# Retention, Fourier mixing and feed-forward on one core: half-height score pairs, and all queues behind the first batch ordered by due times computed in the program text

## Chip, cores and metric

One Trainium2 chip, one core of it. The metric is device time in microseconds (us), fast runs only. Before: 247.51 us, median of 3 (247.45 to 247.79). Engine names as in the profile: PE = TensorE, PEld = its weight loads, DVE = VectorE, ACT = ScalarE, POOL = GpSimd, SP = SyncE, which here issues nearly all the DMAs. A line number such as L1114 is a line of the kernel whose profile is shown; the same statement has another number in each kernel.

## The reference

Four batches, eight heads, 768 rows, heads of 64. Retention with a decayed state, then a two-dimensional Fourier transform (real part), a normalisation, and a feed-forward part of width 2048.

```python
gamma = 1.0 - 2.0 ** (-5.0 - np.arange(H))
for t in range(S):
    state = gamma * state + einsum('bhd,bhe->bhde', k[:, :, t], v[:, :, t])
    y[:, :, t] = einsum('bhd,bhde->bhe', q[:, :, t], state) / np.sqrt(D)
# x: the heads side by side, (4, 768, 512)
u = x + np.real(np.fft.fft(np.fft.fft(x, axis=1), axis=2))
un = (u - mean(u)) / np.sqrt(var(u) + 1e-06)
out = u + np.maximum(un @ w_ch1, 0.0) @ w_ch2          # 512 -> 2048 -> 512
```

## The kernel before

The kernel works on heads in pairs and on rows in six chunks of 128, in fp16 with fp32 sums. While the feed-forward matmuls of one batch run, the retention of the next lies between them. The score unit, with cuts marked:

```python
def a_unit(b, i, part):                      # three parts for each pair of heads
    def run():
        ...                                  # cut: allocation of atm
        wk = ps_g.tile([P, 2, 2, P], f32, tag="g", name="wkA")
        for c2 in range(2):
            c = 2 * part + c2                # qT is zero-padded: both heads in one matmul of 256 columns
            mm = nc.tensor.matmul(wk[:, c2], st["kT"][:, c, :], st["qT"][:, :, c, :], start=True, stop=True)
        nc.vector.tensor_tensor(out=st["atm"][:, 2 * part:2 * part + 2], in0=wk, in1=maskp[...], op=ALU.mult)
```

The casts of batches three and four on GpSimd. `qzs` has two buffers, used in turn, so the cast of the third pair has to wait for the DMA transpose that reads the first pair's buffer, and the fourth for the second:

```python
q16 = qzs[i % 2]
for h2 in range(2):
    nc.gpsimd.tensor_scalar(out=q16[:, h2, :, D * h2:D * h2 + D], in0=q32[:, h2], scalar1=1.0, scalar2=1.0, ...)
...                                          # cut: two casts of k (kd), one of v; later SP transposes q16 to qT
```

The order of the queues comes from the framework's scheduler with hand-set pins:

```python
def pin(engines=None):                       # chain the new instructions of these engines in program order
    for n in range(mark[0], len(ins)):
        ...                                  # cut
        tc.add_manual_dep(x, tails[e], ..., reason="pinned order")
...                                          # cut
...                                          # cut: if e[0] < 1.0, that is, in the first part of the schedule alone
pin(None if e[0] < 0.05 else ["Pool", "GpSimd"])   # first units: all engines; then GpSimd alone
```

Of the kernel before, what the change touches and what calls it, by code (L numbers as in the profile page):

```python
# [31 lines left out]
FB = 1  # L32
NPE = 2
ACT_ROWS = ((2, 5, 6, 7, 8, 9, 10, 14), (0, 3, 6, 7, 9, 10, 11, 12, 14, 15), (2, 4, 5, 6, 7, 8, 10, 14))


@with_exitstack
def kernel(
# [56 lines left out]
    tails, base = {}, {}  # L95
    mark = [0]

    def pin(engines=None):
        ins = tc.nc.cur_bb.bb.instructions
        for n in range(mark[0], len(ins)):  # L100
            x = ins[n]
            e = str(x.engine)
            if engines is not None and not any(g in e for g in engines):
                continue
            if e in tails:
                tc.add_manual_dep(x, tails[e],
                                  mybir.DependencyInfo(mybir.DependencyClass.NoSync,
                                                       mybir.DependencyReason.DATA),
                                  reason="pinned order")
            tails[e] = x.name  # L110
        mark[0] = len(ins)

    def behind():
        for x in tc.nc.cur_bb.bb.instructions[mark[0]:]:
            if str(x.engine) in base:
                tc.add_manual_dep(x, base[str(x.engine)],
                                  mybir.DependencyInfo(mybir.DependencyClass.NoSync,
                                                       mybir.DependencyReason.DATA),
                                  reason="behind the first batch")

    def held(unit):
        def run():
            ins = tc.nc.cur_bb.bb.instructions
            n0 = len(ins)
            unit()
            for n in range(n0, len(ins)):
                m = n - 1
                while m >= 0 and ins[m].engine != ins[n].engine:
                    m -= 1
                if m >= 0:  # L130
                    tc.add_manual_dep(ins[n], ins[m].name,
                                      mybir.DependencyInfo(mybir.DependencyClass.NoSync,
                                                           mybir.DependencyReason.DATA),
                                      reason="casts in turn")
        return run

# [15 lines left out]
    def load_unit(b, i, after=None):  # L152
        def run():
            h0 = 2 * PAIR_ORDER[i]
            for name, src in srcs.items():
                t = inp.tile([P, 2, NCH, D], f32, tag="in32", name=f"{name}32")
                rows = "h (p c) d -> p h c d" if b < NPE and name == "q" else \
                    "h (c p) d -> p h c d"
                dma = nc.sync.dma_start(t, src[b, h0:h0 + 2].rearrange(rows, p=P))  # L159
                if after is not None:  # L160
                    for x in (w_dma[after].ins, lb[0]["mm"].ins):
                        tc.add_manual_dep(dma.ins, x.name,
                                          mybir.DependencyInfo(mybir.DependencyClass.Sync,
                                                               mybir.DependencyReason.DATA),
                                          reason="loads in turn")
                if b > 1:
                    tc.add_manual_dep(dma.ins, a_of[b - 1, 1].ins.name,
                                      mybir.DependencyInfo(mybir.DependencyClass.Sync,
                                                           mybir.DependencyReason.DATA),
                                      reason="loads behind the transposes")  # L170
                in_of[name, b, i] = t
        return run
# [56 lines left out]
    def late_consts():  # L229
        with tc.issue_after(lb[0]["una"].ins):  # L230
            for h in range(H):
                nc.scalar.activation(maskp[:, h // 2, h % 2], maskf, AF.Copy, bias=0.0,
                                     scale=float(gam[h] ** (-P)))
# [119 lines left out]
    at, q16_of, kd_of, v16_of, last_cast = {}, {}, {}, {}, {}  # L353

    def cast_unit(b, i):
        def run():
            h0 = 2 * PAIR_ORDER[i]
            q32, k32, v32 = (in_of.pop((n, b, i)) for n in "qkv")
            kd = kp.tile([P, NCH, 2, D], f16, tag="kd16", name="kd16")
            v16 = vp.tile([P, NCH, 2, D], f16, tag="v16", name="v16")  # L360
            with ExitStack() as es:
                if b < NPE:
                    if (b, i - 1) in last_cast:
                        es.enter_context(tc.issue_after(last_cast[b, i - 1].ins))
                    q16 = qzs[i % 2].rearrange("p h c d -> p (h c d)")[
                        :, 0:NCH * P].rearrange("p (c h d) -> p c h d", c=NCH, h=2)
                    es.enter_context(tc.issue_after(nc.gpsimd.tensor_scalar(
                        out=q16, in0=q32.rearrange("p h c d -> p c h d"), scalar1=1.0,
                        scalar2=1.0, op0=ALU.mult, op1=ALU.mult).ins))
                else:  # L370
                    q16 = qzs[i % 2]
                    for h2 in range(2):
                        dst = q16[:, h2, :, D * h2:D * h2 + D]
                        nc.gpsimd.tensor_scalar(out=dst, in0=q32[:, h2], scalar1=1.0,
                                                scalar2=1.0, op0=ALU.mult, op1=ALU.mult)
                for h2 in range(2):
                    kc = nc.gpsimd.tensor_scalar(out=kd[:, :, h2, :], in0=k32[:, h2],  # L377
                                                 scalar1=gkd[:, h0 + h2:h0 + h2 + 1],
                                                 scalar2=1.0, op0=ALU.mult, op1=ALU.mult)
                    if b < NPE:  # L380
                        es.enter_context(tc.issue_after(kc.ins))
                last_cast[b, i] = nc.gpsimd.tensor_scalar(  # L382
                    out=v16, in0=v32.rearrange("p h c d -> p c h d"), scalar1=1.0, scalar2=1.0,
                    op0=ALU.mult, op1=ALU.mult)
            q16_of[b, i], kd_of[b, i], v16_of[b, i] = q16, kd, v16
        return run
# [25 lines left out]
    def v0_unit(i):  # L412
        def run():
# [3 lines left out]
            last_cast[0, i] = nc.gpsimd.tensor_scalar(  # L417
# [168 lines left out]
    def a_unit(b, i, part):  # L586
        def run():
            st = at[b, i]
            if part == 0:
                st["atm"] = ap_.tile([P, NCH, 2, P], f16, tag="atm", name="atm")  # L590
            wk = ps_g.tile([P, 2, 2, P], f32, tag="g", name="wkA")
            for c2 in range(2):
                c = 2 * part + c2
                mm = nc.tensor.matmul(wk[:, c2], st["kT"][:, c, :], st["qT"][:, :, c, :],  # L594
                                      start=True, stop=True)
            a_of[b, i] = mm
            nc.vector.tensor_tensor(  # L597
                out=st["atm"][:, 2 * part:2 * part + 2], in0=wk,
                in1=maskp[:, PAIR_ORDER[i]].unsqueeze(1).to_broadcast([P, 2, 2, P]),
                op=ALU.mult)  # L600
# [399 lines left out]
    def attn_steps(b):  # L1000
        steps = []
        for step in range(6):
            un = []
            if step < 4:
                un.append(held(cast_unit(b, step)))
# [13 lines left out]
            if 0 <= i < 4:  # L1019
                if b == 0:  # L1020
                    un += [a0_unit(b, i, 0), a0_unit(b, i, 1)]
                else:
                    un += [a_unit(b, i, part) for part in range(3)]
# [62 lines left out]
    def emit(streams):  # L1086
# [5 lines left out]
        for e in ev:  # L1092
            e[3]()
            if e[0] < 1.0:
                behind()
                pin(None if e[0] < 0.05 else ["Pool", "GpSimd"])

    pin()
    for u in first_units():
        u()  # L1100
        pin()
    base.update(tails)
# [4 lines left out]
    for b in range(B):  # L1107
# [14 lines left out]
        dm = (0.12, 0.24, 0.3, 0.38) if b == 0 else (0.004, 0.140, 0.232, 0.341)  # L1122
        streams += [(majors, b, b + 1.0), (s2s, b + dm[0], b + dm[1]),
                    (unTs, b + dm[2], b + dm[3])]
        if b + 1 < B:
            steps = attn_steps(b + 1)
            if b == 0:
                streams.append(([load_unit(1, i, 6) for i in range(4)], 0.180, 0.220))
                streams.append(([qt_zeros], 0.1, 0.15))
                streams.append(([half_tables], 0.655, 0.655 + 0.02))  # L1130
                streams.append(([pad_unit], 0.673, 0.703))
                ts = (0.249, 0.368, 0.410, 0.415, 0.507, 0.615, 0.680, 0.685)
            else:
                streams.append(([load_unit(b + 1, i) for i in range(4)], b + -0.370, b + 0.075))
                n = [len(u) for u in steps[1:]]
                ts = [-0.040, -0.020] + [0.050 + 0.585 * sum(n[:j]) / sum(n)
                                         for j in range(6)]
# [3 lines left out]
            da = (0.062, 0.080, 0.173, 0.203, 0.271, 0.321) if b == 0 else \  # L1141
                (0.063, 0.067, 0.048, 0.158, 0.168, 0.189)
# [4 lines left out]
    emit(streams)  # L1147

# [29 lines left out]
```

## Time and profile before

| | before |
|---|---|
| time, median of fast runs | 247.65 us (4 runs of the same rounds as after) |
| span of the profiled run, mean granted clock | 246.0 us, 1.000 |
| PE busy | 234.4 us, 95% |
| PE time lost against each matmul form's median interval | 14.8 us, of it 9.9 before 36 us and 5.0 behind |

The last row is read from the start times of single matmuls: interval from one start to the next, less the median interval of the same form, added up where it is above 40 ns. It counts waits, mode switches and half-speed stretches alike, and is the measure used below.

The prediction shows the page and the stages. One more stage matters for what followed, the change from batch three to batch four, here on the timelines of POOL and SP (columns: start, length, engine, line, operation, tiles, shapes, count, and in brackets the idle time before and what ended it):

```profile
140.03 0.64 POOL L866 TENSOR_TENSOR u<-u,x 128x256 f32<-128x256 f32 x1
140.64 0.98 POOL L374 TENSOR_SCALAR q16z<-q 128x384 f16<-128x384 f32 x2
```

```profile
137.86 3.61 SPq L910 DMA_TRANSPOSE unT<-un  x2
141.65 1.44 SPq L542 DMA_TRANSPOSE qTz<-q16z  x1
```

The reader is to see two orders. POOL does the additions that end batch three's transform (u) first and batch four's next q cast afterwards. SP transposes batch three's normalised rows (unT), which the feed-forward part waits for, ahead of batch four's heads (qTz).

### The profile page before, as it was taken

The numbers are of one execution on the slowest core, as the hardware profiler recorded it, in microseconds if no ns is written. First come the engines' busy times: TensorE is split into PE (matmuls) and PEld (weight loads), VectorE is DVE, ScalarE is ACT, GpSimd is POOL, SyncE is SP. The second block draws the span as 40 slices with busy tenths as digits, with TensorE's granted clock in tenths as the row PEclk, the third lists the DMA queues.
The fourth block names the chain that finished last, engine by engine and source line by source line (L and its number), as shares of the span: only waits on it lengthen the run. The fifth ranks groups of instructions, "written<-read, shape, count | busy, mean of one in ns | idle before, by whom it ended". The sixth has DMA issues, their size and how long they took to land.

```text
span 246.0 us, 5309 instructions
## 1 busy us (share of the span) xinstructions
PE 234.4 (95%) x2024; PEld 144.4 (59%) x2024; DVE 177.5 (72%) x430; ACT 124.3 (51%) x276; POOL 81.3 (33%) x146
## 2 busy tenths in 40 slices
PE   6897899999999999999999999999999998999994
PEld 2454668956676655665567446665666455445543
DVE  8998957898788788995987648887895657424122
ACT  8798669477785445742247415732257217202500
POOL 6667600376500068690001637660003214000000
PEclk9999999999999999999999999999999999999999
DMA  8998999699999287988999589596100331121012
GB/s 174 257 260 138 200 204 206 152 250 261 275 233 214 56 171 176 190 174 149 242 266 210 119 183 181 108 138 150 58 0 3 60 133 30 38 85 43 0 45 85
DMA packets 99209, 36.39 MB, mean 148 GB/s; under 512 B 89840, under 2 KB 96240, under 8 KB 99184
## 3 DMA queue, kind: packets, MB, share of 16 engines
q1 hardware_dynamic: 94960, 31.86, 62.5%
q0 software_dynamic: 4224, 4.19, 10.5%
q8 instruction: 16, 0.26, 0.5%
q14 instruction: 9, 0.07, 0.1%
HBM read 27.26 MB, written 6.29 MB: 136 GB/s over the span
## 4 chain that ended last, share of the span: by engine, by line
PE 72%; DVE 8%; POOL 7%; ACT 4%; SPq 3%; DMA 2%; issue 2%; POOLq 0%; DVEq 0%
PE psc L973 30%; PE psh L930 23%; SPq L159 3%; PE ps L730 3%; PE psh L947 3%; PE wkA L594 3%; DMA k<-in_k_dram 2%; PE wkY L648 2%; POOL u L864 2%; POOL u L866 2%; PE wkY L644 1%; DVE bst L883 1%; PE wkK L613 1%; DVE u L834 1%; PE pq L827 1%
## 5 line engine op out<-in xcount | busy, mean ns | idle before, releaser
L973 PE MATMUL psc<-w,ht 128*128 128x512 f16 (+1 forms) x400 | 89.6, 370 | 0.1
L930 PE MATMUL psh<-unT,w 128*128 128x384 f16 x448 | 81.3, 326 | 0.6 <-ACT ht L934 0.6
L973 PEld LDWEIGHTS <-ht 128*128 128x128 f16 x400 | 38.1, 98 | 35.5 <-issue 0.3
L930 PEld LDWEIGHTS <-w 128*128 128x128 f16 x448 | 42.3, 98 | 24.9 <-issue 1.3
L934 ACT ACTIVATE ht<-psh 128x384 f16<-128x384 f32 x64 | 30.6, 488 | 39.4 <-PE psh L930 38.3
L864 POOL TENSOR_TENSOR u<-u,x 128x256 f32<-128x256 f32 x21 | 13.3, 634 | 102.3 <-DVE u L834 90.7
L977 DVE SCALAR_TENSOR_TENSOR ob<-psc,stats,u 128x512 f32<-128x512 f32 (+1 forms) x25 | 18.1, 722 | 27.4 <-PE psc L973 27.3
L936 DVE TENSOR_SCALAR ht<-psh 128x384 f16<-128x384 f32 x48 | 26.3, 551 | 8.6 <-PE psh L930 8.3
L597 DVE TENSOR_TENSOR atm<-wkA,maskp 128x512 f16<-128x512 f32 x36 | 23.9, 685 | 1.0 <-PE wkA L594 1.0
L885 ACT ACTIVATE un<-u,stats 128x512 f16<-128x512 f32 x21 | 15.1, 721 | 16.9 <-DVE stats L884 8.7
L883 DVE BATCH_NORM_STATS2 bst<-u 128x6 f32<-128x512 f32 x21 | 14.6, 694 | 9.7 <-POOL u L866 9.5
L623 DVE SCALAR_TENSOR_TENSOR s<-s,gk,wkK 128x128 f16<-128x128 f16 x48 | 16.4, 343 | 2.3 <-ACT s L619 1.4
L656 ACT ACTIVATE x<-wkY,gexp 128x384 f16<-128x384 f32 x24 | 12.8, 580 | 9.3 <-PE wkY L648 9.3
L145 PE MATMUL wps<-ht 128*128 128x512 f16 x40 | 13.3, 439 | 2.2 <-POOL ht L196 2.2
L377 POOL TENSOR_SCALAR kd<-k,gexp 128x384 f16<-128x384 f32 x24 | 13.8, 584 | 2.4 <-DMA k<-in_k_dram 2.4
L866 POOL TENSOR_TENSOR u<-u,x 128x256 f32<-128x256 f32 x21 | 13.3, 634 | 2.8 <-DVE u L837 1.5
L594 PE MATMUL wkA<-qTz,kT 128*128 128x256 f16 x72 | 13.6, 273 | 0.0
L829 ACT COPY qn<-pq 128x128 f32<-128x128 f32 x18 | 4.9, 274 | 14.1 <-PE pq L827 13.9
L947 PE MATMUL psh<-unT,w 128*128 128x128 f16 x192 | 11.5, 219 | 0.1
L947 PEld LDWEIGHTS <-w 128*128 128x128 f16 x192 | 11.0, 98 | 0.7 <-issue 0.5
L382 POOL TENSOR_SCALAR v<-v 128x768 f16<-128x768 f32 x12 | 10.0, 830 | 2.0 <-DMA v<-in_v_dram 1.9
L594 PEld LDWEIGHTS <-kT 128*128 128x128 f16 x72 | 6.9, 98 | 6.0 <-DVE s L623 0.4
(164 smaller groups left out, 318.2 us busy)
## 6 DMA issues: line engine op xcount, KB each, us to landing
q<-in_q_dram SPq DMA_DIRECT2D x16, 384.0 KB, 6.2
k<-in_k_dram SPq DMA_DIRECT2D x16, 384.0 KB, 5.6
v<-in_v_dram SPq DMA_DIRECT2D x16, 384.0 KB, 6.6
out_dram<-ob SPq DMA_DIRECT2D x23, 256.0 KB, 2.6
w<-in_moe_w_ch_dram POOLq DMA_DIRECT2D x8, 512.0 KB, 11.1
out_dram<-ob SPq DMA_DIRECT2D x2, 128.0 KB, 1.7
unT<-un SPq DMA_TRANSPOSE x15, 2.4
qTz<-q16z SPq DMA_TRANSPOSE x8, 3.8
```

The source lines that it names most:

```text
L594: mm = nc.tensor.matmul(wk[:, c2], st["kT"][:, c, :], st["qT"][:, :, c, :], start=True, stop=True)
L597: nc.vector.tensor_tensor(out=st["atm"][:, 2 * part:2 * part + 2], in0=wk, in1=maskp[:, PAIR_ORDER[i]].unsqueeze(1).to_broadcast([P, 2, 2, ...
L623: nc.vector.scalar_tensor_tensor(out=s16[:, c], in0=s16[:, c - 1], scalar=gk2[:, hp:hp + 1], in1=wk[:, c - c0], op0=ALU.mult, op1=ALU.add)
L864: nc.gpsimd.tensor_tensor(out=u[:, kb, 0:256], in0=u[:, kb, 0:256], in1=x[:, kb, 0, 1:257], op=ALU.add)
L866: nc.gpsimd.tensor_tensor(out=u[:, kb, 256:512], in0=u[:, kb, 256:512], in1=x[:, kb, 1, 257:1:-1], op=ALU.add)
L883: nc.vector.bn_stats(bst, u[:, kb, :])
L930: nc.tensor.matmul(psh, w116[:, cb, fb * P:(fb + 1) * P], unT[:, cb, rt * 384:(rt + 1) * 384], start=(cb == 0), stop=(cb == 3))
L934: nc.scalar.activation(ht16[:, fb, :], psh, AF.Relu, bias=0.0, scale=-1.0)
L936: nc.vector.tensor_scalar(out=ht16[:, fb, :], in0=psh, scalar1=-1.0, scalar2=0.0, op0=ALU.mult, op1=ALU.max)
L947: mm = nc.tensor.matmul(psh[:, f], w116[:, cb, fb * P:(fb + 1) * P], unT[:, cb, kb * P:(kb + 1) * P], start=(cb == 0), stop=(cb == 3))
L973: nc.tensor.matmul(psc[:, c0:c1], ht16[:, fb, rb3 * P:(rb3 + 1) * P], w216[:, fb, c0:c1], start=(fb == 0), stop=(fb == NFB - 1))
L977: nc.vector.scalar_tensor_tensor(out=ob[:, c0:c1], in0=psc[:, c0:c1], scalar=lb[b]["st"][:, rb, 3:4], in1=lb[b]["u"][:, rb, c0:c1], op0=AL ...
```

## The change

Two intents. First, the scores of two heads become two concurrent matmuls of 64 rows: a pair of them takes 52 to 56 ns from start to start in the traces, a zero-padded matmul of 256 columns 109 ns. Second, the hand-set pins go; the program text itself gives each instruction a cost and a due time, worked backwards from PE's program order, simulates the five queues and pins the order that comes out. With the second goes a set of new tables (LD1 and others) of where in the program each unit of work stands; no run tried these alone. The core of the diff, the rest cut:

```diff
+SLACK = 12000.0
+BY_DUE = ('PE', 'DVE', 'Activation', 'Pool', 'SP')
+def instr_cost(x, PSUM=PSUM):
+    ...                                     # cut
+    if eng == "PE":
+        ...                                 # cut: n columns written; half, if an operand has at most 64 rows
+        return max(n / 2.4 + 2.5, 27.0) * (0.5 if half else 1.0), n / 2.4 + 165.0
+    if kind == "InstDMACopy":
+        return (780.0 if eng == "Pool" else 400.0), None       # time the issuing engine is taken, ns
+    if kind == "InstDmaTransposeAnt":
+        return 1400.0, 3800.0 if el > 600 else 2450.0
+    ...                                     # cut
+def order_queues(tc, told, kept):
+    ...                                     # cut: who needs whom; due times backwards
+    rank = [(due[n] if eng[n] in BY_DUE else float(n), n) for n in range(len(ins))]
+    ...                                     # cut: simulated queues take the ready instruction of lowest rank
+            rate = 205.0 if e == "Pool" else 225.0 if runs[-1][1] <= 64 else 340.0
+            dma = max(dma, t + 1300.0) + 4.0 * size / rate
+            end = dma + 600.0
+    ...                                     # cut: every queue is pinned to that order
-    def pin(engines=None): ...              # and behind(), held(): removed
     def a_unit(b, i, part):                 # now two parts for each pair
-            wk = ps_g.tile([P, 2, 2, P], f32, tag="g", name="wkA")
-            for c2 in range(2):
-                c = 2 * part + c2
-                mm = nc.tensor.matmul(wk[:, c2], st["kT"][:, c, :], st["qT"][:, :, c, :], ...)
+            wk = [ps_g.tile([P, 3, P], f32, tag="g", name="wkA", padded_shape=[P, 4, P]) for _ in range(2)]
+            for c3 in range(3):
+                c = 3 * part + c3
+                for h2 in range(2):
+                    sl = slice(D * h2, D * h2 + D)
+                    mm = nc.tensor.matmul(wk[h2][:, c3, :], st["kT"][sl, c, :], st["qT"][sl, h2, c, :], ...)
```

## The prediction

> **What bounds the kernel now.** In the names, psh and psc are the two layers of the feed-forward part and fill most of PE's time; tq are transposes, wkA scores, wkK states, wkY the attention's output; ps, pq the Fourier part; pst turns the normalised un into unT. I read the page first, then the windows view cut at the stages, then groups by shape, the PE timeline, and the start times of single matmuls.
>
> ```profile
> PE 234.4 (95%) x2024; PEld 144.4 (59%) x2024; DVE 177.5 (72%) x430; ACT 124.3 (51%) x276; POOL 81.3 (33%) x146
> PE 72%; DVE 8%; POOL 7%; ACT 4%; SPq 3%; DMA 2%; issue 2%; POOLq 0%; DVEq 0%
> ```
>
> TensorE is busy 95% of the span and has 72% of the chain that ended last. The stages say it more sharply:
>
> ```profile
> 41.20:59.00 17.80, 17.80 (x211) 13.42 (x211) 14.92 (x43) 12.57 (x23) 9.92 (x15) 1.00 1.04 215
> 59.00:82.50 23.50, 23.28 (x246) 15.26 (x244) 20.21 (x46) 15.04 (x29) 4.89 (x8) 1.00 1.12 230
> 82.50:135.00 52.50, 51.98 (x442) 32.91 (x440) 43.42 (x109) 25.23 (x60) 19.31 (x33) 1.00 0.95 184
> 135.00:187.50 52.50, 52.10 (x415) 31.54 (x414) 40.07 (x96) 22.70 (x54) 18.82 (x33) 1.00 0.56 111
> 187.50:243.00 55.50, 54.62 (x312) 29.69 (x310) 23.56 (x49) 15.84 (x38) 7.02 (x12) 1.00 0.18 56
> ```
>
> The first two numbers are the length and PE's busy time: behind the first batch 199.8 of 201.8 us. Taking each matmul's start to the next one's start, and the median of its form as its cost, I find 4.2 us of lost time in that stretch. So order alone can win 4.2 us at the very most, plus about 1 us at 34 to 41 us. A win of 2% is 5 us. Two of the losses:
>
> ```profile
> 95.12 0.44 PE L613 MATMUL wkK<-v,kd 128*128 128x128 f16 x5 [0.47 <-POOL v L382]
> 208.03 3.41 PE L930 MATMUL psh<-unT,w 128*128 128x384 f16 x20 [0.44 <-ACT ht L934]
> ```
>
> **What the Trainium skill says.** "TensorEngine Tiling (Array Packing)", Key Properties: a change of tiling mode drains TensorE. The trace agrees. The first batch already forms its scores with 64-row matmuls, between full-height fillers:
>
> ```profile
> 17.87 0.60 PE L145 MATMUL wps<-ht 128*128 128x512 f16 x2
> 18.41 0.51 PE L458 MATMUL wkA<-qTz,kT 64*128 64x128 f16 x12
> 18.85 0.39 PE L145 MATMUL wps<-ht 128*128 128x512 f16 x1
> ```
>
> Fillers follow each other at 216 ns, so two take 0.43 us, but the 64-row burst starts 0.54 us after them: single starts show 312 ns in place of 216, so 96 ns on entry, in two bursts alike (others enter 96 to 97 ns late behind other forms). On leaving, the next matmul starts 149 ns after the last half matmul where 53 is its own time: 96 ns again. The first pair and the first filler lose 10 ns more each. "TensorE: Matmul & The Clock Gate", The mechanism (part 3): matmuls in different row groups start some 4 ns apart and all matmuls keep program order. The trace agrees: the partners start 3 to 4 ns apart, pairs 52 to 56 ns apart. The same page, Architectural detail, says that ScalarE and VectorE are strict FIFO; nothing in the trace contradicts it, and the stages below rest on it.
>
> **Part 1, half-height pairs.** Removed: 72 full-height matmuls.
>
> ```profile
> L594 PE MATMUL wkA<-qTz,kT 128*128 128x256 f16 x72 | 13.6, 273 | 0.0
> L597 DVE TENSOR_TENSOR atm<-wkA,maskp 128x512 f16<-128x512 f32 x36 | 23.9, 685 | 1.0 <-PE wkA L594 1.0
> ```
>
> The 13.6 us include overlap; from start to start one takes 109 ns, together 7.9 us. Added: 144 of half height, 72 pairs. At 53 ns a pair and nothing else, 3.8 us: 4 us saved, which the new cost function in the program assumes (half the time, no switch). But the built order shows where they stand: in batch two three bursts of 12, one of 6 and two of 3 matmuls; in batches three and four sixteen bursts of 6, each between full-height matmuls. A burst costs 56 ns a pair plus 0.21 us for the switches: 0.55 us (12), 0.38 (6), 0.32 (3, two pair slots). Sum: 3 x 0.55 + 17 x 0.38 + 2 x 0.32 = 8.75 us. **Part 1 costs about 0.9 us** on the path. The evictions become 48 of 384 columns in place of 36 of 512; 685 less 128 columns at about 1 ns makes 0.55 us each, 26 us in place of 24: DVE is beside the path, no charge.
>
> **Part 2, the order at 48 to 66 us.** In the new program all 48 psc matmuls of the first half of batch one stand before the first transposes (tq) of batch two; before, 20 stood ahead and the rest lay between them. They go in fours by the w2 load that they need, and the reason is in the program text: its cost function charges each weight load 4 bytes x 262144 / 205 = 5.1 us. The trace has the packets of those eight loads at 2.6 to 3.7 us each, done at 44.8 us, and the batch-two loads start right behind:
>
> ```profile
> SPq L159 <- DMA w<-in_moe_w_ch_dram: 26.0, 1, 26.0
> 44.97 0.37 SPq L159 DMA_DIRECT2D q<-in_q_dram  x1
> ```
>
> So the order is built around a shortage that isn't there. The psc end at 48.7 + 48 x 0.216 + 0.2 = 59.3 us. Then the queue has only dependent work: ACT must do, in its order, qTz twice, kT, s, qTz twice, kT, unT of block five, and only then can psh run.
>
> ```profile
> 57.58 1.61 ACT L556 COPY qTz<-tq 64x768 f16<-64x768 f16 x2 [0.18 <-PE tq L550]
> 59.21 0.80 ACT L561 COPY kT<-tq 128x768 f16<-128x768 f16 x1
> 59.90 0.27 ACT L619 CAST s<-wkK 128x128 f16<-128x128 f32 x1
> ```
>
> 2 x (1.61 + 0.80) + 0.27 + 0.58 = 5.7 us from 59.9, so 65.6. PE has for that time 24 tq and 8 pst (56 ns), 10 wkK (56 ns), 12 half wkA (0.55) and some wkY (0.23): 3.2 us. Stall 65.6 - 59.3 - 3.2 = 3.1 us, where the old order loses 0.7 us to 77 us. **+2.4.** The fold behind it has less filler (12 psc and 2 psh in place of 10 and 9): **+0.3.**
>
> **Part 3, batch changes at 90 and 145 us.** In the new order SP issues all 12 loads of batch three before that batch's first DMA transpose, and POOL's third q cast, which needs that transpose done, stands before the u additions of batch two. [...]
>
> ```profile
> 69.38 1.70 SPq L159 DMA_DIRECT2D q<-in_q_dram  x1
> 71.17 2.27 SPq L159 DMA_DIRECT2D k<-in_k_dram  x1
> ```
>
> The cost function takes 0.4 us each. The loads wait for wkA of the second pair, 65.3 us before and about 69 now (from 65.6, 12 psh at 162 ns, 12 tq and the burst: 3.2 us); at some 1.7 us each SP is free at 88 to 89, the transpose lands near 94, the additions end near 99 in place of 92.2, and the first psh of batch two waits 2 to 3 us where the old order loses 0.9. I extrapolate here, so I charge half: **+1.0.** The same pattern (fourth q cast before the additions) recurs one batch later with 10 us of psc in between: 0 to 4 us, I charge **+0.6.**
>
> **What it gains.** Casts of two pairs now precede the additions, which removes the wait for POOL v at 95 us (already counted in the net above) and likely that at 156 us (0.7). At the end, DVE and ACT take ht ahead of the statistics: of the 1.2 us lost at 205 to 211 perhaps 0.8. **-1.5.** Sum: 247.5 + 0.9 + 2.4 + 0.3 + 1.0 + 0.6 - 1.5 = 251.2; I go a little lower, 250.6, because the many times in the text look tuned.
>
> **Rivals.** A: the switches hide in this setting and order also removes the 4 us lost: 247.5 - 4 - 3 = 240.5. For it: clean pairs at 53 ns. Against: the same drain on the five entries and three exits that I looked at, and the stall at 59 us, which follows from order and measured durations. B: part 1 neutral, order evens out: 246 to 248, if the late stages gain all of their 3 us and the transposes come early enough. C: the batch changes cost in full, twice: 254 to 257; for it, SP's issue times; against, DMA may be faster with fewer outputs in between.
>
> **Range and chances.** B to C gives 246 to 256. Faster than 242.6 needs A, against direct evidence: 0.05. Slower than 252.5 needs most of C: 0.33. Else 0.62.
>
> **What would show it.** Half-height wkA with entry and exit 96 ns late, some 8.7 us in all; PE idle of about 3 us between 59 and 66 us with ACT busy on qTz and kT; POOL waiting for a DMA transpose near 90 us while PE waits at pst; fewer gaps at 205 to 211. I am wrong in part 1 if half-height bursts start without delay, and in part 2 if psh runs on without a gap at 60 us.

## The result, and the profile after

After: **265.72 us**, median of 4 (264.52 to 266.12); before, on the same chip, 247.65 (247.45 to 247.88). The ratio is 1.072, with a 95% interval of 1.069 to 1.075. Ratios are the mean time of one kernel's fast runs over that of the other's fast runs of the same rounds, so not quite the ratio of the medians quoted. The result is correct, all runs are of the fast state. It is slower by 18 us; predicted was 250.6, at most 256.

The page of the kernel after, its busy times and the chain that ended last:

```profile
PE 238.1 (90%) x2096; PEld 142.0 (54%) x2096; DVE 178.9 (68%) x442; ACT 124.5 (47%) x276; POOL 83.5 (32%) x146
...
PE 68%; DMA 8%; DVE 7%; ACT 6%; SPq 6%; POOL 3%; issue 2%; POOLq 0%; ACTq 0%; DVEq 0%
```

PE is busy for more us but a smaller share; the chain now has DMA with 8% and SP's queue with 6% where it had 2% and 3%. The windows of the kernel after, cut at about the same events as the prediction's (columns: window, length, busy us of PE, PEld, DVE, ACT, POOL with counts, granted clock, DMA share, GB/s):

```profile
41.20:61.20 20.00, 18.95 (x200) 13.06 (x198) 13.16 (x38) 8.29 (x20) 9.26 (x14) 1.00 1.02 202
61.20:87.00 25.80, 23.61 (x276) 15.85 (x274) 20.04 (x48) 19.44 (x35) 12.72 (x18) 0.93 0.96 200
87.00:150.00 63.00, 58.50 (x504) 33.97 (x503) 48.10 (x121) 26.76 (x65) 19.64 (x32) 1.00 0.90 169
150.00:170.00 20.00, 11.70 (x60) 5.63 (x58) 6.63 (x15) 3.18 (x7) 8.29 (x14) 0.83 0.50 125
170.00:205.80 35.80, 35.80 (x344) 21.32 (x342) 31.44 (x80) 17.15 (x38) 4.87 (x8) 1.00 0.30 67
```

The fourth row is the news: in 20 us PE is busy for 11.7, at a granted clock of 0.83. In the fifth row, and behind it, PE is busy almost throughout and loses little but the mode switches. The lost time of PE by stage, in us, read as explained above (each kernel's stages are cut at its own batch events):

| stage | before | after | more | predicted term |
|---|---|---|---|---|
| first batch, to 36 us | 9.9 | 9.7 | -0.2 | none |
| first layers, to 50 us | 0.7 | 2.4 | +1.7 | none |
| batch two's attention, to about 80 us | 0.7 | 4.8 | +4.1 | +2.4 |
| transform and batch change at 85 to 110 us | 1.2 | 5.8 | +4.5 | +0.3, +1.0 |
| to about 147 us | 0.2 | 1.7 | +1.6 | part 1 |
| batch change at 150 to 170 us | 0.8 | 9.9 | +9.1 | +0.6 |
| the rest | 1.3 | 1.4 | +0.1 | less switches -1.5 |
| sum | 14.8 | 35.7 | +20.9 | |

Every row after the second also holds its share of the mode switches, 45 of 95 to 98 ns, 4.3 us in all, of which 3 lie in the first batch (before: 4, all there); the differences are taken before rounding. The span grew by 18.3 us and not by 20.9, mainly because the half-height matmuls take some 4 us less time of their own (72 pairs at 53 ns against 7.9 us); the rest lies in differences under the 40 ns. Their group after:

```profile
L778 PE MATMUL wkA<-qTz,kT 64*128 64x128 f16 x144 | 8.7, 221 | 1.4 <-DVE s L807 0.6 <-ACT kT L741 0.4 <-ACT qTz L736 0.4
```

**The stage at 60 us**, two of the waits on PE and then ACT of the kernel after, answers to the three ACT lines in the prediction:

```profile
63.65 0.38 PE L1098 MATMUL pst<-ident,un 128*128 128x128 f16 x4 [0.33 <-ACT kT L741]
65.31 0.42 PE L778 MATMUL wkA<-qTz,kT 64*128 64x128 f16 x6 [0.39 <-ACT qTz L736]
```

```profile
61.16 1.61 ACT L736 COPY qTz<-tq 64x768 f16<-64x768 f16 x2 [6.59 <-PE tq L730]
...
63.65 1.61 ACT L736 COPY qTz<-tq 64x768 f16<-64x768 f16 x2
```

ACT had been idle for 6.6 us, as PE's queue held the transposes back behind 48 output matmuls, and then does qTz, kT, qTz, kT in a row with PE waiting at each step. Behind these waits the granted clock is 0.5 from 65.85 us for 3.41 us.

**The stage at 157 us**, SP, POOL and PE of the kernel after, against the timelines of before:

```profile
143.30 1.68 SPq L345 DMA_DIRECT2D v<-in_v_dram  x1
...
146.84 2.06 SPq L722 DMA_TRANSPOSE qTz<-q16z  x1
...
159.56 1.19 SPq L1094 DMA_TRANSPOSE unT<-un  x1
```

```profile
152.10 0.99 POOL L556 TENSOR_SCALAR q16z<-q 128x384 f16<-128x384 f32 x2 [11.98 <-DMA qTz<-q16z]
...
155.34 0.99 POOL L556 TENSOR_SCALAR q16z<-q 128x384 f16<-128x384 f32 x2 [0.31 <-POOL v L563]
156.29 0.64 POOL L1048 TENSOR_TENSOR u<-u,x 128x256 f32<-128x256 f32 x1
```

```profile
146.62 10.52 PE L1157 MATMUL psc<-w,ht 128*128 128x512 f16 x48
165.44 3.48 PE L1114 MATMUL psh<-unT,w 128*128 128x384 f16 x12 [8.30 <-DMA unT<-un]
```

The same two steps on PE of the kernel before, without a gap:

```profile
136.31 10.52 PE L973 MATMUL psc<-w,ht 128*128 128x512 f16 x48
146.66 1.46 PE L930 MATMUL psh<-unT,w 128*128 128x384 f16 x8
```

The kernel after is to be read backwards. PE waits 8.3 us for the transposed rows (unT). SP could issue that transpose at 159.56 only, since the rows were not normalised; POOL's first addition for them starts at 156.29, because the casts of the third pair and the q casts of the fourth stand ahead of it in POOL's queue. The cast at 152.10 had kept POOL idle for 11.98 us: it needs a head transpose that SP issued at 146.84, behind 12 loads, the last issued at 143.30. From 161.42 us the clock is at half for 6.83 us; most of that lies inside the wait, and only the last 2.8 us meet running matmuls, a loss of some 1.4 us. The same pattern gives 3.75 us at 98 us.

### The profile page after: what moved, and what is told of

It is laid out like the page before. It is cut to its first block, busy times and chain, and to the rows that moved or that the text cites. A ratio compares the mean times of both kernels' runs of the same rounds, so it can differ in the third digit from the quotient of the medians.

```text
span 264.3 us, 5451 instructions
## 1 busy us (share of the span) xinstructions
PE 238.1 (90%) x2096; PEld 142.0 (54%) x2096; DVE 178.9 (68%) x442; ACT 124.5 (47%) x276; POOL 83.5 (32%) x146
## 4 chain that ended last, share of the span: by engine, by line
PE 68%; DMA 8%; DVE 7%; ACT 6%; SPq 6%; POOL 3%; issue 2%; POOLq 0%; ACTq 0%; DVEq 0%
PE psh L1114 28%; PE psc L1157 25%; SPq L345 4%; PE ps L914 3%; DMA q<-in_q_dram 3%; DMA qTz<-q16z 3%; PE wkA L778 2%; DMA unT<-un 2%; PE wkY L832 2%; PE wkY L828 1%; PE wkK L797 1%; ACT qTz L736 1%; PE pq L1011 1%; DVE bst L1067 1%; ACT un L1063 1%
## 5 line engine op out<-in xcount | busy, mean ns | idle before, releaser
L1114 PE MATMUL psh<-unT,w 128*128 128x384 f16 x448 | 83.2, 331 | 8.4 <-DMA unT<-un 8.3
L1157 PE MATMUL psc<-w,ht 128*128 128x512 f16 (+1 forms) x400 | 87.7, 371 | 0.1
L1114 PEld LDWEIGHTS <-w 128*128 128x128 f16 x448 | 41.5, 99 | 33.9 <-issue 10.5
L1118 ACT ACTIVATE ht<-psh 128x384 f16<-128x384 f32 x64 | 31.3, 491 | 57.6 <-PE psh L1114 57.0
L782 DVE TENSOR_TENSOR atm<-wkA,maskp 128x384 f16<-128x384 f32 x48 | 24.0, 549 | 1.9 <-PE wkA L778 1.5
L556 POOL TENSOR_SCALAR q16z<-q 128x384 f16<-128x384 f32 x16 | 8.5, 546 | 42.9 <-DMA qTz<-q16z 23.1
L560 POOL TENSOR_SCALAR kd<-k,gexp 128x384 f16<-128x384 f32 x24 | 15.2, 642 | 18.4 <-PE wkK L797 9.8
L1018 DVE SCALAR_TENSOR_TENSOR u<-pq,g,qn 128x256 f32<-128x256 f32 x18 | 8.6, 478 | 5.4 <-PE psh L1114 4.5
L1131 PEld LDWEIGHTS <-w 128*128 128x128 f16 x192 | 11.0, 98 | 1.5 <-issue 1.5
L921 ACT CAST g<-ps 128x386 f16<-128x386 f32 x14 | 7.8, 599 | 5.6 <-PE ps L914 5.4
```

Of the source, the lines that this page charges most:

```text
L560: nc.gpsimd.tensor_scalar(out=kd[:, :, h2, :], in0=k32[:, h2], scalar1=gkd[:, h0 + h2:h0 + h2 + 1], scalar2=1.0, op0=ALU.mult, op1=ALU.mult)
L782: nc.vector.tensor_tensor(out=st["atm"][:, 3 * part:3 * part + 3, h2, :], in0=wk[h2], in1=maskp[:, hp, h2].unsqueeze(1).to_broadcast([P, 3 ...
L1114: nc.tensor.matmul(psh, w116[:, cb, fb * P:(fb + 1) * P], unT[:, cb, rt * 384:(rt + 1) * 384], start=(cb == 0), stop=(cb == 3))
L1118: nc.scalar.activation(ht16[:, fb, :], psh, AF.Relu, bias=0.0, scale=-1.0)
L1131: mm = nc.tensor.matmul(psh[:, f], w116[:, cb, fb * P:(fb + 1) * P], unT[:, cb, kb * P:(kb + 1) * P], start=(cb == 0), stop=(cb == 3))
L1157: nc.tensor.matmul(psc[:, c0:c1], ht16[:, fb, rb3 * P:(rb3 + 1) * P], w216[:, fb, c0:c1], start=(fb == 0), stop=(fb == NFB - 1))
```

## The experiments

All 15 runs gave a correct result. For each the median time is quoted, and beside it the ratio to the kernel before in the same rounds; before was at 247.45 to 247.72 us in all of them. My theory was: the orders cost the time, above all SP's loads and POOL's casts ahead of the additions, and the half-height pairs cost almost nothing. The rivals were that the pairs are the main cause, that SP's loads hold everything up whatever POOL does, and that the lower clock is a cause rather than a consequence.

**1. Half-height pairs on the old orders.** The a_unit of the diff above in the kernel before, nothing else.

> The kernel before with one part of the change alone: the score pairs of batches two to four half height, in two parts of six matmuls, old queue orders otherwise. Theory (the orders cost the time, the half-height pairs almost nothing): 24 bursts, each with a switch of 96 ns in and out (the trace of the changed kernel shows 95 to 97 ns), 4.6 us, against some 5.5 us less matmul time than the full-height pairs (each full-height burst of two 256-column matmuls against the concurrent halves); with the score work on VectorE cut into other pieces I expect 246.5 to 250 us, within 1.5% of before. Rival (half-height switches or the new evictions are the main cause): 255 us or more. Rival of the change's author (switches hidden): 242 us or less.

Measured: 251.26 us, ratio 1.015 (1.014 to 1.016). So the pairs cost 3.7 us here, neither almost nothing nor the main cause. The score matmuls took 7.98 us from start to start before; they now take 7.53 us, which holds the switches on leaving and one wait of 0.4 us. The trace has them in 26 bursts (two of the 24 are split by other matmuls), so 26 entries of 96 ns come to it: without the wait 9.6 us, so 1.6 us of the 3.7. The rest are waits, of which the largest on PE's timeline of this run is for a score eviction on VectorE:

```profile
160.82 0.26 PE L652 MATMUL wkY<-v,atm 128*128 128x64 f16 x3 [0.79 <-DVE atm L602]
```

**2. One burst for each pair, old orders.**

```diff
+            wks = [[ps_g.tile([P, 3, P], ...) for _ in range(2)] for _ in range(2)]
+            for c in range(NCH):            # all twelve matmuls, then four evictions
```

> As the run with half-height pairs alone, but the twelve matmuls of a pair in one burst (four PSUM tiles taken at once), so 12 bursts in place of 24. If a burst costs two switches of 96 ns and PE is the bound, this is 12 x 0.19 = 2.3 us shorter than the run with two bursts a pair; if the switches are hidden it is equal; if taking four PSUM buffers at once makes TensorE wait for their evictions it is slower than that run by up to 3 us.

Measured: 254.25 us, ratio 1.027 (1.024 to 1.030), 3.0 us slower than two bursts. The switches fell from 51 to 33, but the bursts were split again by waits for PSUM inside them, 1.2 us at 103 us and 2.4 us at 157 us, ended by VectorE. The third of the three expectations held.

**3. Two casts moved behind the additions, batch four only.** All other queues keep the order of the kernel after.

```diff
+MOVES = ((18, 23, 18),)     # the fourth pair's two q casts go behind batch three's sixth addition
+        moved = [n for n in casts[late:late + 2] if pool_q.index(n) < last]
+        ...                                  # cut: take them out of the queue
+        at_ = pool_q.index(adds[last_add]) + 1
+        pool_q[at_:at_] = moved
```

> The changed kernel with one thing moved: in GpSimd's queue, the two q casts of batch four's fourth pair stand behind the six u additions of batch three's end and no longer ahead of the last of them. All other queues keep their order. Theory (the wait of 8.5 us at 156.8 us comes from the q casts, which wait for the transpose of the pair two earlier to read the buffer, which SP issues only behind 12 loads): the wait falls to 1 us or less and the half clock after it goes too, so 8 to 10 us shorter, 256 to 258 us. Rival 1 (the loads hold up SP and the transposes themselves stop TensorE a little later): the wait reappears at batch four's first scores or states, 3 us or less gained. Rival 2 (the lower clock comes from power and not from the wait): the clock falls to half near 161 us all the same and 2 to 3.4 us of the loss stay.

Measured: 264.73 us, ratio 1.070 (1.067 to 1.073). Only 1 us was gained, and the intervals overlap with those of the kernel after (1.069 to 1.075), so the expectation of 8 to 10 us failed. POOL's timeline of this run shows why, and that the experiment had missed its aim:

```profile
151.11 0.99 POOL L572 TENSOR_SCALAR q16z<-q 128x384 f16<-128x384 f32 x2 [11.96 <-DMA qTz<-q16z]
...
153.99 0.64 POOL L1064 TENSOR_TENSOR u<-u,x 128x256 f32<-128x256 f32 x1
```

It is the third pair's cast that waits, and I had left it in front. At this point the rival (SP alone holds the chain) was not refuted.

**4. The same, and the third pair's casts at the batch change before.**

> As the run that moves the two casts, and the same at the batch change before: the q casts of batch three's third pair go behind batch two's last u addition in GpSimd's queue. Theory: the wait of 3.75 us near 98 us goes as well, 3 to 4 us below the run with one move, 252 to 255 us. Rival (the wait at 98 us is set by the loads and not by the cast): within 1 us of that run.

Measured: 261.18 us, ratio 1.056 (1.051 to 1.061): 3.5 us below the run before, as the theory said. At this batch change the third pair's casts were the ones moved, and the wait of 3.75 us at 98 us is gone.

**5. The additions ahead of the third pair's casts, at both changes.**

```diff
+MOVES = ((6, 12, 8), (18, 24, 16))
+    for first, last, cast in MOVES:
+        front = pool_q.index(casts[cast])
+        moved = [n for n in adds[first:last] if pool_q.index(n) > front]
+        ...                                  # cut: take them out of the queue
+        pool_q[front:front] = moved
```

> The run that moved two casts missed its aim: in its trace the wait at 156 us is still 7.1 us, because the casts of the third pair (GpSimd at 151.11, idle 11.96 us before them for the transpose of the first pair's q) also stand ahead of the additions. Here the six u additions of each batch change go ahead of the third pair's q casts, at both batch changes; all else is the changed kernel. Theory: the additions then run at 146 to 149 us; the transposes of the normalised rows are issued by SP behind the fourth head transpose at about 153.5 us and land at 156, so TensorE's wait at 156 us falls from 8.5 us to at most 1 us, the half clock behind it goes, the wait at 98 us goes too: 249 to 254 us. Rival (SP alone holds the chain: loads until 145 us, then four head transposes, whatever GpSimd does): a wait of 3 us or more stays at 156 us, 256 us or more.

Measured: 256.28 us over all four runs, ratio 1.032 (1.024 to 1.040) over the three fast ones: 253.74, 255.38 and 257.18 us; the fourth, 258.46, counts as slow. Moving six additions in one queue, twice, gains some 9 to 10 us. SP and PE of this run:

```profile
142.45 1.86 SPq L736 DMA_TRANSPOSE qTz<-q16z  x1
...
150.14 2.53 SPq L1108 DMA_TRANSPOSE unT<-un  x2
```

```profile
156.05 2.11 PE L1128 MATMUL psh<-unT,w 128*128 128x384 f16 x12 [2.63 <-DMA unT<-un]
```

The wait fell from 8.3 to 2.6 us, not to 1: SP still issues the rows' transposes behind four head transposes. So both were right in part, POOL for most of it and SP for the rest. The half clock behind this wait is gone, and POOL's order was all that was changed: here the lower clock followed from the wait and was no cause of its own.

**6. Full-height pairs on the new orders.** The old a_unit in the kernel after. The program text computes the queues anew from the costs, here and in runs 7 to 15, so an edit can move instructions anywhere.

> The changed kernel's due-time orders with the score pairs at full height as before: the other half of the change alone. If the orders are the loss and half-height pairs cost 3.7 us on the old orders, this is about 265.7 - 3.7 = 262 us. If the two parts do not add, because the new order's waits hide the switches, it is 265 to 266. If the half-height pairs are what makes the orders go wrong (other pieces, other due times), it is 255 us or less.

Measured: 269.2 us, ratio 1.088 (1.084 to 1.091). Slower than with half-height pairs, which none of the three cases foresaw. Its trace has the wait at 157 us at 10.5 us (8.5 after) and half-clock stretches behind both batch changes. It settles that the half-height pairs are not what makes the orders go wrong.

**7. One number of the cost function: SP's issue of a load.**

```diff
-        return (780.0 if eng == "Pool" else 400.0), None
+        return (780.0 if eng == "Pool" else 1700.0), None
```

> The changed kernel with one number of its cost function changed: issuing a load from SP costs 1700 ns in place of 400 ns (the traces show 1.6 to 1.8 us each where several stand in a row). Theory: the program text then knows that the head transposes of a new batch are issued late and puts the u additions and the transposes of the normalised rows ahead of them by itself; the waits at 98 and 157 us shrink below 2 us each: 252 to 257 us. Rival (other figures of the cost function, such as the landing of transposes and loads, are as wrong): the waits move but stay, 260 us or more.

Measured: **253.46 us**, ratio 1.024 (1.022 to 1.025), 12.3 us less than the kernel after. SP and PE of this run:

```profile
147.20 2.50 SPq L1094 DMA_TRANSPOSE unT<-un  x2
149.80 1.46 SPq L722 DMA_TRANSPOSE qTz<-q16z  x1
```

```profile
143.99 10.52 PE L1157 MATMUL psc<-w,ht 128*128 128x512 f16 x48
154.35 0.40 PE L1011 MATMUL pq<-gk,g16r 128*128 128x129 f16 x4
```

The program text now puts the rows' transposes ahead of the heads' by itself, as the kernel before did, and after 48 output matmuls PE goes on without a gap. This is the main cause, shown by changing that one number: the cost function took an issue of SP for 0.4 us, where loads in a row take 1.6 to 1.8 us. Printed from the program text of the kernel after, the simulated queues have the first head transpose of batch four issued at 131.2 us; the trace has it at 146.84. What paces the issues was not tested. In the trace of the kernel after the first loads of a row take 0.4 to 0.8 us to issue; the ten from 127.95 us on take 17.1 us, and ten times 384 KB in that time are some 230 GB/s by my estimate, where the window shows 220 GB/s moved. So the 1.7 us may be the pace of the data and not the price of an issue, and may differ for loads of another size.

**8. Another number: the rate of the weight loads**, 390 in place of 205.

> The changed kernel with one number of its cost function changed: the rate charged for the weight loads of GpSimd's queue, 390 in place of 205, so about 2.7 us for a load as in the trace and not 5.1. The cost function then lets batch two's loads and first transposes come earlier, as the chip does. Theory: the stage from 59 to 70 us loses its waits (some 4 us with the half clock behind them) and the first stage near 38 to 48 us its three gaps (2.4 us): 259 to 262 us. Rival (that stage is set by the order of ActivationE's and VectorE's evictions whatever the loads): 264 to 267 us.

Measured: 268.55 us, ratio 1.086 (1.080 to 1.091): slower by about 3 us. The expected effect is there, as transposes now stand between the output matmuls and there is no half clock at 65 us, but the batch changes got worse (waits of 3.0 and 1.2 us at 96 to 102 us, 9.4 us at 157 us).

**9. Both numbers.**

> Both numbers of the cost function corrected: 1700 ns for SP's issue of a load and 390 for the rate of the weight loads. The run with the second alone took the waits at 59 to 70 us down (excess of TensorE's intervals up to 80 us 15.2 us against 17.7 us, no half clock there) but kept the waits at both batch changes (3 + 1.2 us at 96 to 102 us, 9.4 us at 157 us). If the two act in separate stages, the sum holds: 253.5 less about 3, so 250 to 251.5 us. If they do not (the weight rate moves batch two's loads and with them the later stages), 253 us or more.

Measured: 250.94 us, ratio 1.012 (1.011 to 1.014). On top of the issue cost the same number gains 2.5 us, while alone it lost 3. The reason that the prediction gave for the order at 48 to 66 us, the rate charged to the weight loads, holds.

**10. The issue cost, with full-height pairs.**

> The issue cost corrected (1700 ns) and the score pairs at full height again: beside the run with the issue cost alone this is the half-height part by itself, on orders without the long waits. If half-height pairs cost what they cost on the old orders (3.7 us), 249.8 us; if only the switches count against the saved matmul time (my first accounting, +0.9 us), 252.5 us; if they gain, as the run of the uncorrected orders at full height suggests (269.2 against 265.7), 255 us or more.

Measured: 252.74 us, ratio 1.020 (1.018 to 1.022), 0.7 us below run 7. With the long waits gone, half-height pairs lose 0.7 us, near my first accounting of 0.9; but this run has one wait of 1.5 us that run 7 lacks, and run 7 a stretch at half clock, so the 0.7 is no clean price of the pairs.

**11. PE's and DVE's queues between 51 and 70 us mended**, on top of run 7.

```diff
+    forward(pe_q, tq[0], 21, "psc", 28)      # pair one: transposes, rows, states ahead of 28 output matmuls
+    forward(pe_q, tq[12], 12, "psc", 8)      # pair two's transposes ahead of the last 8
+    forward(dve_q, unt, 5, "ob_", 3)         # a copy and four state updates ahead of three evictions
```

> The issue cost corrected, and in the stage of 51 to 70 us alone: in TensorE's queue the first pair's transposes, the row transposes and its state products (21 matmuls) stand ahead of the last 28 of the 44 output matmuls, the second pair's transposes ahead of the last 8, and VectorE's copy and state updates go ahead of three output evictions. Theory (ActivationE is idle 6.6 us and VectorE 4.3 us there because TensorE's queue holds the transposes back, and then both evict in a row while TensorE waits): TensorE's waits of 3.3 us and the half clock behind them go, 3 to 4.5 us shorter than with the issue cost alone: 249 to 250.5 us. Rival (the evictions are the bound and the wait only moves): less than 1.5 us gained.

Measured: **249.85 us**, ratio 1.008 (1.007 to 1.010), 3.6 us below run 7. ACT, then PE, of this run:

```profile
55.03 1.61 ACT L763 COPY qTz<-tq 64x768 f16<-64x768 f16 x2 [0.55 <-PE tq L757]
...
60.52 1.61 ACT L763 COPY qTz<-tq 64x768 f16<-64x768 f16 x2 [2.89 <-PE tq L757]
```

```profile
63.49 0.63 PE L824 MATMUL wkK<-v,kd 128*128 128x128 f16 x5 [0.17 <-ACT unT L1132]
```

ACT's copies of the first pair start 6 us earlier and lie beside the output matmuls; what PE still waits there is one idle of 0.17 us and a few tenths more. The granted clock is 1.0 throughout.

**12 to 15. What is left.** Run 12 moves an eviction on ACT and small transform matmuls on PE at three places with waits of about 1 us each; 13 is the same with full height, 14 with one burst for each pair; 15 is 14 with more moves of that kind at 42 to 46 and at 84 us.

```diff
+    forward(act_q, act_q[k], 1, "qn", 2)     # run 12: an eviction ahead of two copies
+    back(pe_q, ps0[0], 9, "psc", 4)          # nine small matmuls behind four output matmuls
+    back(pe_q, ps1[36], 12, "psh", 4)        # twelve behind four hidden-layer matmuls
```

> The run with TensorE's queue mended between 51 and 70 us still shows waits of 1.0 us at 43 us (an eviction on ActivationE behind three copies), 1.1 us at 83 us and 0.9 us at 134 us (small matmuls of the transform ahead of matmuls that were ready). Here the eviction goes ahead of two of the copies, the nine small matmuls at 83 us behind four output matmuls, twelve at 134 us behind four hidden-layer ones. Theory (what is left over before is such waits and the switches): some 2 to 2.5 us of the 3.0 us go, 247.2 to 248.2 us, so level with before. Rival (VectorE and ActivationE are the bound there and the waits come back later): 249 us or more.

> As the run with the three moves more, with full-height pairs. With the issue cost alone full height was 0.7 us shorter than half height, though it had one wait of 1.5 us more at 152 us. Theory: 0.7 us below the run with half-height pairs, 246.5 to 247.5 us. If its own waits (at 152 us and others) grow, 248 us or more.

> As the run with the three moves more, with the twelve half-height matmuls of a pair in one burst (four PSUM tiles at once). Switches: about 12 in place of about 22 bursts, so 10 x 0.19 = 1.9 us less on TensorE: 245.5 to 246.5 us if the evictions come free in time. On the old orders this form was 3 us slower than two bursts a pair, its trace having waits inside the bursts of 0.5 to 2.4 us for PSUM; if the due-time orders do not cure that, 248.5 us or more.

> The last attempt at a version below before: the run with one burst a pair, plus two evictions of VectorE ahead of four updates and two statistics in the stage of 42 to 46 us, ActivationE's eviction ahead of three copies in place of two, and five more output matmuls ahead of the small matmuls at 84 us. Its trace has waits of 0.85, 0.32 and 0.50 us in the first stage and of 0.39 and 0.84 us at 84 us. Theory: some 2 us of these 2.9 us go, 246.3 to 247.3 us, just below before. Rival, as in the run with three moves: they come back later, because VectorE and ActivationE have as much to do as before, 248 us or more.

Measured: 249.57 us, ratio 1.007 (1.006 to 1.008); 250.37, 1.013 (1.010 to 1.017); 248.51, 1.004 (1.003 to 1.005); 248.71, 1.005 (1.004 to 1.006). Run 12 gained 0.3 us of the 2 hoped for, less than the intervals can tell apart. The waits came back: 1.1 us at 83 us became 0.4 and 0.8 us at 85 us, with VectorE as the releaser. In run 13 a wait of 3.4 us appeared at 149 us; its trace is of the slowest of the six runs, 252.82 us, with a stretch at half clock behind that wait. Run 14 fits the switches as a cost of their own: the traces have 16 bursts against 22 in run 12, so 12 switches fewer, 12 x 0.096 = 1.2 us, and 1.1 us were gained. In run 15 what was taken away at 44 us returned as a wait of 1.6 us at 47 us for an eviction on VectorE. No version beat the kernel before.

## Why the prediction was wrong

**What bounds the kernel.** Right: order could win little, and nothing was won. The lost time behind 36 us was 5.0 us before and no order tried came below it.

**Part 1, half-height pairs, +0.9.** The mechanism is right: 96 ns on entry and 96 on leaving, wherever no wait covers it. The sum of the bursts was right too: in run 11, which has the same 22 bursts and no long wait among them, they take 8.8 us with their switches where 8.75 was worked out, and 8.0 us before. What this costs in the end is not settled at one number: about +0.7 us on orders with the issue cost corrected, +3.7 on the old orders. There the bursts are 26 and take 9.6 us, and "DVE is beside the path, no charge" failed, since PE waited for score evictions.

**Part 2, order at 48 to 66 us, +2.4.** Right in mechanism, with ACT's row of copies as told, and in its reason (run 9). Mending it gave 3.6 us. The working had the waits (3.1 us of stall; PE's waits from 61.7 to 66.1 us add up to 3.0), and left out the stretch at half clock behind them: 3.41 us at half speed lose up to 1.7 us.

**The stage before it, no term.** 1.7 us of waits between 38 and 48 us were missed: the prediction has no term for them.

**Fold filler, +0.3.** One wait of 1.0 us at 87 us, against 0.3 before. Too small by about 0.4 us.

**Part 3, batch changes, +1.0 and +0.6.** This is the step that failed. The mechanism was in the text, step for step the chain of the trace: 12 loads, then the head transpose, then POOL's cast, then the additions, with 0.4 us charged for issues that take 1.7. But its terms were sized by "I extrapolate here, so I charge half" and "with 10 us of psc in between: 0 to 4 us". Measured: a wait of 3.75 us at the first change, where 2 to 3 us had been worked out and then halved, and one of 8.3 us at the second; with the transform stage, half clock and switches +4.5 and +9.1 us of lost time. Correcting the issue cost alone takes 12.3 us away. The block of psc does lie in between, 10.5 us from 146.62, but SP is occupied with loads until 145 us and POOL with two pairs of casts until 156 us, and the rows still need additions, normalisation and a transpose of 2.5 us after that, so the block covers 10.5 us of a chain that takes 18.8. I had also named the fourth pair's cast alone as the obstacle; the third pair's is the one that waits 12 us, which run 3 showed by failing. Carrying the same issue times on to batch four, as was done for batch three, would have given a wait well above 4 us; this is reckoned afterwards.

**Gains, -1.5.** Right. The waits of 0.4, 0.6 and 0.2 us at 205 to 211 us and the two at 156 us are gone.

**The rivals.** C (batch changes in full, twice) was the right one, and its 254 to 257 still had the second change too small. A and B did not occur.

**Left open.** The 2.1 us between run 11 and before. The waits in it move when the queues are changed, and DVE is the releaser of several; that VectorE's work is the limit there is argued, not shown. Nor is it shown why full-height pairs are slower than half-height ones on the uncorrected orders, nor what the new tables of places do by themselves: every run with computed orders has them.

## What to carry to other kernels

A computed order is as good as the cost of the engine that is least looked at: one number for the issue of a load, 0.4 us where the chip took 1.7, cost 12 us, and the check is to lay the times that the cost function believes beside the trace, queue by queue. A producer that waits on a buffer must not stand ahead of ready work on the path in a strict queue (runs 4 and 5). And a mechanism seen to recur is charged at each place with that place's own times, not at half.

## What the Trainium skill lacked or had wrong

- "TensorEngine Tiling (Array Packing)", Key Properties, says that a change of tiling mode drains TensorE but gives no price: here 95 to 98 ns on entry and again on leaving, 45 times in the trace after; and a form with 12 fewer of them was 1.1 us faster (run 14 against run 12).
- "TensorE: Matmul & The Clock Gate", Part 1, says that the clock is full or half and is set by free-running windows of 3413 ns, falling after an idle one. The trace agrees on the sizes: 0.5 for 3.41 and for 6.83 us, one and two windows. Its tie to an idle window is too narrow here: the clock fell at 65.85 us with no single wait above 0.72 us, six of them adding up to 3.0 us between 61.7 and 66.1 us, and in run 8 it fell at 98.79 us, though PE had stood idle for only 2.2 of the 3.41 us before. The wait of 3.75 us at 98 us brought no fall in the profiled run; counted in steps of 3.41 us from 65.85 us, it lies across two windows and fills neither, so that this one fits the page. (A later section of the page does say that short idle times between groups can throttle, without a number.) In run 5 the four times 253.74, 255.38, 257.18 and 258.46 us go with mean clocks of 1.000, 0.993, 0.986 and 0.979: steps of 1.3 to 1.8 us, each about one window at half speed.
- "DMA: Bandwidth & Descriptors", Anatomy of one DMA, calls the cost of generating descriptors small and variable (for the GpSimd path) and has no time for which SP is taken by an issue on this chip (a table on a later chip has a cycle count for "previous generations"): here SP is held 0.4 us for a first load of 384 KB, 1.6 to 1.8 us for each of those behind it (up to 3.1), and 1.2 to 2.7 us for a DMA transpose.
- No page that I read treats the order of loads and transposes on one issuing queue: loads and one output ahead of a head transpose held SP from 126.59 to 146.84 us.
